# An RWKV-6 scan with a SoLU MLP on one core: exponentials kept in PSUM, the bonus term moved to GpSimd and TensorE, y copied by ScalarE

## The chip, the cores and the metric

The kernel runs on one core of one Trainium2 chip. The metric is the device time of one execution in microseconds (us). Five engines work side by side, each through its own queue in program order: TensorE (PE; its weight loads are listed as PEld), VectorE (DVE), ScalarE (ACT), GpSimd (POOL) and SyncE (SP), which here only sends DMAs. They wait for each other through semaphores.

## The reference

Two stages. The first is a linear attention with a decay per channel, over batch 4, 8 heads, 768 steps and head size 48:

```python
for t in range(S):
    cur = u * k[t] (outer) v[t]
    y[t] = r[t] @ (state + cur)
    state = w[t][:, None] * state + k[t] (outer) v[t]
```

The second takes the 3072 rows of y (384 wide, all heads side by side) through an MLP:

```python
h = x @ w_in                       # 384 -> 1024
solu = h * softmax(h)
ln = (solu - mean) / sqrt(var + 1e-6) * g_ln
out = ln @ w_out                   # 1024 -> 384
```

The term with u is the bonus: for each step and head it is the scalar sum over d of r*u*k, times v.

## The kernel before, in words

The sequence is cut into chunks of 128 steps. A unit is one chunk of one batch entry with all eight heads: 24 units, numbered c*4 + b, so that a state (one per batch entry) is read and written by every fourth unit. Each unit goes through a chain of stages, and the loop over t emits the stages of five neighbouring units together. The functions are emitted in the order of that loop, but the order in which instructions stand on each engine is made by a scheduler; the rows in the section on the change come from the built programs.

The stages of unit i, by function:

- `load(i)`: four DMAs of 192 KB bring w, k, r, v (f32) from SP's queue. The pool `io` holds five of each.
- `decay(i)`: ScalarE takes log w (`lw`, L128), TensorE cumulates it over the 128 steps by two triangular matrices into the PSUM tile `cum_ps` (L130, L131), and ScalarE writes the exponential of both halves to the SBUF tile `ex` in bf16 (L133).
- `scaled(i)`: VectorE multiplies k and r by the two halves, giving `kp` and `rp` (L140, L141).
- `bonus(i)`: GpSimd casts v to bf16 (`vb`, L147), and makes p = r*k (L149) and q = p*u (L151); VectorE sums q over each head (`dg`, L153) and makes `dv` = vb times dg (L155).
- `transposed(i)`: TensorE transposes kp and rp into `kr_ps`, VectorE copies them to `kr` (L165).
- `scores(i)`: TensorE makes k-by-r products in `m_ps` (L175), ScalarE copies them to `m` (L177), GpSimd masks them to the strict triangle (L178).
- `attend(i)`: TensorE sums into `y_ps` the read of the state (L190) and m times vb (L194); VectorE adds dv and writes `y` (L198).
- `state(i)`: TensorE forms the new state in `s_ps` (last matmul L220), ScalarE the decay `et` (L223), VectorE writes `st` (L228).
- `x_transposed(i)` and `hidden(i)`: y is transposed (`x_ps`, `xT`, L237), 24 matmuls make `h_ps` (L246), ScalarE makes e = exp(h) (L249), VectorE he = h*e (L251).
- `output(i)`: TensorE sums he times the prepared second weights into `o_ps` (L261, L264), and he times he into `g_ps` (L263). The statistics follow as a chain of small steps: `sq` on ScalarE (L267), `junk` with its accumulated `ss` on VectorE (L270), `qm` = ss - sq on VectorE (L272), `lv` = log and `rs` = exp(-lv/2) on ScalarE (L274, L276), and the scaled copy `o` (L278), which a DMA on SP's queue stores (L279).

PSUM has eight banks here: the pool `big` has two tiles of two banks, taken in turn by cum_ps, h_ps and m_ps; the pool `small` has four of one bank, taken by kr_ps, y_ps, o_ps, g_ps, x_ps and s_ps. Most SBUF tiles of a stage have three buffers (pool `wk`). Ahead of the loop the constants and the first units are loaded, and `setup_weights` prepares the second weights `w2`: 16 f32 matmul passes (L115) and eight VectorE instructions (L119), after the small DMA of g (`g_sb`, L102) has landed.

Of the kernel before, what the change touches and what calls it, by code (L numbers as in the profile page):

```python
# [9 lines left out]
BF16 = mybir.dt.bfloat16  # L10
AX = mybir.AxisListType.X
EXP = mybir.ActivationFunctionType.Exp
# [8 lines left out]
def kernel(  # L21
# [12 lines left out]
    nc = tc.nc  # L34
    B, H, S, D = r.shape
    C = 128
    NC = S // C
    DM = H * D
# [12 lines left out]
    wk = ctx.enter_context(tc.tile_pool(name="wk", bufs=3))  # L51
# [6 lines left out]
    def load(i):  # L58
        c, b = units[i]
        for name, src in (("w", w), ("k", k), ("r", r), ("v", v)):  # L60
            t = io.tile([C, H, D], F32, tag=name + "_in", name=name + "_in")
            nc.sync.dma_start(out=t, in_=src[b, :, c * C:(c + 1) * C, :].rearrange("h t d -> t h d"))  # L62
            live[i][name] = t
# [12 lines left out]
    ident = consts.tile([C, C], BF16)  # L76
# [14 lines left out]
    for b in range(B):  # L91
        nc.vector.memset(st_t[b], 0.0)

    u_bc = consts.tile([C, H, D], F32)
    nc.sync.dma_start(out=u_bc, in_=u.partition_broadcast(C))
    load(1)
    win_sb = consts.tile([128, KM, DF], BF16)
    nc.gpsimd.dma_start(out=win_sb, in_=moe_w_in.rearrange("(ko ki) f -> ki ko f", ki=128))
    wout_f = consts.tile([128, KF, DM], F32)
# [24 lines left out]
    def decay(i):  # L124
        L = live[i]
        lw = lw_t[i % NR]
        L["lw"] = lw
        nc.scalar.activation(out=lw[:, :, :D], in_=L["w"], func=LN)  # L128
        cum = big.tile([C, 2, 512], F32, tag="b", name="cum_ps")
        nc.tensor.matmul(cum[:, 0, :DM], lhsT=uti_neg, rhs=lw[:, :, :D], start=True, stop=True)  # L130
        nc.tensor.matmul(cum[:, 1, :DM], lhsT=uts, rhs=lw[:, :, :D], start=True, stop=True)  # L131
        ex = wk.tile([C, 2, DM], BF16, tag="ex", name="ex")
        nc.scalar.activation(out=ex, in_=cum[:, :, :DM], func=EXP)  # L133
        L["ex"] = ex

    def scaled(i):
        L = live[i]
        kp, rp = kp_t[i % NR], rp_t[i % NR]
        ex = L["ex"].rearrange("t e (h d) -> t e h d", h=H)
        nc.vector.tensor_mul(out=kp[:, :, :D], in0=L["k"], in1=ex[:, 0])  # L140
        nc.vector.tensor_mul(out=rp[:, :, :D], in0=L["r"], in1=ex[:, 1])  # L141
        L["kp"], L["rp"] = kp, rp

    def bonus(i):
        L = live[i]
        vb = wk.tile([C, H, D], BF16, tag="vb", name="vb")
        nc.gpsimd.tensor_copy(out=vb, in_=L["v"])  # L147
        p = wk.tile([C, H, D], BF16, tag="p", name="p")
        nc.gpsimd.tensor_mul(out=p, in0=L["r"], in1=L["k"])  # L149
        q = wk.tile([C, H, D], BF16, tag="q", name="q")  # L150
        nc.gpsimd.tensor_mul(out=q, in0=p, in1=u_bc)  # L151
        dg = wk.tile([C, H], F32, tag="dg", name="dg")
        nc.vector.reduce_sum(out=dg, in_=q, axis=AX)  # L153
        dv = wk.tile([C, H, D], BF16, tag="dv", name="dv")
        nc.vector.tensor_mul(out=dv, in0=vb, in1=dg.unsqueeze(2).to_broadcast([C, H, D]))  # L155
        L["vb"], L["dv"] = vb, dv

    def transposed(i):
# [23 lines left out]
    def attend(i):  # L182
        L = live[i]
        c, b = units[i]
        m, kr, vb, st = L["m"], L["kr"], L["vb"], st_t[b]
        y_ps = small.tile([C, DM], F32, tag="s", name="y_ps")
        first = True
        if c > 0:
            for hp in range(HP):
                nc.tensor.matmul(y_ps[:, hp * 2 * D:(hp + 1) * 2 * D], lhsT=kr[:, HP + hp, :], rhs=st[:, hp, :],  # L190
                                 start=first, stop=False, skip_group_check=True)
                first = False
        for h in range(H):
            nc.tensor.matmul(y_ps[:, h * D:(h + 1) * D], lhsT=m[:, h % 2, h // 2, :], rhs=vb[:, h, :],  # L194
                             start=first, stop=(h == H - 1), skip_group_check=True)
            first = False
        y = wk.tile([C, DM], BF16, tag="y", name="y")
        nc.vector.tensor_add(out=y, in0=y_ps, in1=L["dv"].rearrange("t h d -> t (h d)"))  # L198
        L["y"] = y

    def state(i):
# [52 lines left out]
    def output(i):  # L254
        L = live[i]
        c, b = units[i]
        e, he = L["e"], L["he"]
        o_ps = small.tile([C, DM + 2], F32, tag="s", name="o_ps")
        g_ps = small.tile([C, C], F32, tag="s", name="g_ps")
        for f in range(KF):  # L260
            nc.tensor.matmul(o_ps[:, :DM + 1], lhsT=he[:, f, :], rhs=w2[:, f, :], start=(f == 0), stop=False,  # L261
                             skip_group_check=True)
            nc.tensor.matmul(g_ps, lhsT=he[:, f, :], rhs=he[:, f, :], start=(f == 0), stop=(f == KF - 1))  # L263
            nc.tensor.matmul(o_ps[:, DM + 1:], lhsT=e[:, f, :], rhs=inv_col, start=False, stop=(f == KF - 1),  # L264
                             skip_group_check=True)
        sq = wk.tile([C, 2], F32, tag="sq", name="sq")
        nc.scalar.activation(out=sq, in_=o_ps[:, DM:], func=SQUARE)  # L267
        junk = wk.tile([C, C], BF16, tag="junk", name="junk")
        ss = wk.tile([C, 1], F32, tag="ss", name="ss")
        nc.vector.scalar_tensor_tensor(out=junk, in0=g_ps, scalar=1.0, in1=ident, op0=MULT, op1=MULT, accum_out=ss)  # L270
        qm = wk.tile([C, 1], F32, tag="qm", name="qm")
        nc.vector.tensor_sub(out=qm, in0=ss, in1=sq[:, 0:1])  # L272
        lv = wk.tile([C, 1], F32, tag="lv", name="lv")
        nc.scalar.activation(out=lv, in_=sq[:, 1:2], func=LN, scale=1e-6 * DF * DF, bias=qm)  # L274
        rs = wk.tile([C, 1], F32, tag="rs", name="rs")
        nc.scalar.activation(out=rs, in_=lv, func=EXP, scale=-0.5)  # L276
        o = io.tile([C, DM], F32, tag="o", name="o")
        nc.scalar.activation(out=o, in_=o_ps[:, :DM], func=COPY, scale=rs)  # L278
        nc.sync.dma_start(out=out[b * S + c * C:b * S + (c + 1) * C, :], in_=o)  # L279
# [5 lines left out]
    for t in range(NU + LAST):  # L285
        on = lambda d: 0 <= t - d < NU
        if t + LOOK < NU:
            load(t + LOOK)
        if on(0):
            decay(t)  # L290
            bonus(t)
        if on(3):
            hidden(t - 3)
        if on(0):
            scaled(t)
        if on(1):
            transposed(t - 1)
        if on(2):
            attend(t - 2)
        if on(4):  # L300
            output(t - 4)
        if on(1):
            scores(t - 1)
        if on(2):
            x_transposed(t - 2)
            state(t - 2)
        if t == 1:
            setup_weights()
# [30 lines left out]
```

## Time and profile before

| | |
|---|---|
| median of 3 runs | 214.92 us (214.33 to 215.04) |
| profiled execution, its own time | 214.99 us |
| its span, first to last instruction | 213.3 us |
| VectorE busy | 161.3 us (76%) |
| TensorE busy | 153.5 us (72%) |
| ScalarE busy | 104.8 us (49%) |
| GpSimd busy | 93.7 us (44%) |

The profile is of one execution, so its 214.99 us are what its rows are summed against. They stand 0.07 us above the median. A busy time counts how long instructions ran, also while they were held up by something inside, so a busy share says which engines are candidates and not which one sets the pace. The chain of waits (which follows the last instruction back to what released each step) and the timelines of single engines tell that.

### The profile page before, as it was taken

What the parts mean: (1) busy time and instruction counts of PE and PEld (TensorE: products, weight loads), DVE (VectorE), ACT (ScalarE), POOL (GpSimd) and SP (SyncE); (2) the same over time, 40 slices, a digit from 0 to 9 for tenths busy, and PEclk for the clock granted to TensorE, in tenths of its full rate; (3) what the DMA queues carried; (4) which work ended last, traced back from release to release, by engine and by line L of the source; (5) the groups of instructions that cost most, each with busy time, mean ns of one, the idle gap of its engine ahead of it and who ended that gap; (6) DMA issues with size and microseconds to landing.
All of it is one profiled execution on the core that took longest, in us unless ns stands there. A gap on an engine that the chain in (4) does not pass through costs nothing.

```text
span 213.3 us, 5315 instructions
## 1 busy us (share of the span) xinstructions
PE 153.5 (72%) x2120; PEld 120.5 (57%) x2120; DVE 161.3 (76%) x338; ACT 104.8 (49%) x213; POOL 93.7 (44%) x108
## 2 busy tenths in 40 slices
PE   1031790758788877976987897897788889899970
PEld 0010450647676655864865576676567767687660
DVE  3037349899989989878888898798898787985420
ACT  3031010445564665474376455547545666665652
POOL 4049254458645364473274367256436331322200
PEclk9999997599799999998899997999996999999999
DMA  6999999992457979786765675485561001010102
GB/s 124 219 200 267 181 182 187 190 175 54 92 94 160 190 139 185 160 167 124 163 148 119 139 150 125 86 173 125 114 148 40 32 11 40 37 39 37 40 37 75
DMA packets 105944, 26.49 MB, mean 124 GB/s; under 512 B 101312, under 2 KB 105536, under 8 KB 105920
## 3 DMA queue, kind: packets, MB, share of 16 engines
q1 hardware_dynamic: 105520, 25.37, 59.5%
q0 software_dynamic: 400, 0.79, 2.0%
q8 instruction: 16, 0.26, 0.5%
q14 instruction: 8, 0.07, 0.1%
HBM read 22.22 MB, written 4.72 MB: 126 GB/s over the span
## 4 chain that ended last, share of the span: by engine, by line
DVE 38%; PE 19%; SPq 12%; issue 10%; ACT 9%; DMA 6%; POOL 3%; POOLq 1%; DVEq 0%; ACTq 0%
SPq L62 10%; DVE he L251 9%; PE h_ps L246 6%; DVE rp L141 6%; PE o_ps L261 5%; DVE kp L140 4%; DVE kr L165 4%; DMA r_in<-in_r_dram 4%; DVE y L198 3%; DVE w L119 2%; DVE dg L153 2%; ACT m L177 2%; DVE st L228 2%; DVE qm L272 2%; DVE dv L155 2%
## 5 line engine op out<-in xcount | busy, mean ns | idle before, releaser
L261 PE MATMUL o_ps<-w,he 128*128 128x385 bf16 x192 | 50.2, 329 | 1.1 <-DVE he L251 1.1
L263 PE MATMUL g_ps<-he 128*128 128x128 bf16 x192 | 41.9, 220 | 0.0
L246 PE MATMUL h_ps<-xT,win_sb 128*128 128x128 bf16 x576 | 40.7, 233 | 0.0
L147 POOL CAST vb<-v_in 128x384 bf16<-128x384 f32 x24 | 12.5, 520 | 63.9 <-PE s_ps L220 54.3
L246 PEld LDWEIGHTS <-win_sb 128*128 128x128 bf16 x576 | 38.5, 106 | 3.4 <-issue 1.0
L178 POOL TENSOR_SCALAR_AFFINE_SELECT m<-m 128x1024 bf16<-128x1024 bf16 x24 | 27.6, 1150 | 23.2 <-ACT m L177 23.0
L149 POOL TENSOR_TENSOR p<-r_in,k_in 128x384 bf16<-128x384 f32 x24 | 25.1, 1047 | 16.5 <-DMA r_in<-in_r_dram 15.6
L249 ACT ACTIVATE e<-h_ps 128x1024 bf16<-128x1024 f32 x24 | 24.6, 1025 | 15.2 <-PE h_ps L246 14.9
L264 PE MATMUL o_ps<-inv_col,e 128*128 128x1 bf16 x192 | 32.0, 167 | 0.0
L251 DVE TENSOR_TENSOR he<-h_ps,e 128x1024 bf16<-128x1024 f32 x24 | 29.1, 1214 | 3.7 <-ACT e L249 3.6
L130 PE MATMUL cum_ps<-lw,uti_neg 128*128 128x384 bf16 x24 | 8.4, 351 | 31.6 <-ACT lw L128 31.4
L177 ACT CAST m<-m_ps 128x1024 bf16<-128x1024 f32 x24 | 24.0, 999 | 13.8 <-PE m_ps L175 13.8
L151 POOL TENSOR_TENSOR q<-p,u_bc 128x384 bf16<-128x384 bf16 x24 | 26.2, 1095 | 1.6
L140 DVE TENSOR_TENSOR kp<-k_in,ex 128x384 bf16<-128x384 f32 x24 | 16.4, 685 | 13.3 <-ACT ex L133 13.1
L264 PEld LDWEIGHTS <-e 128*128 128x128 bf16 x192 | 18.7, 97 | 13.1 <-issue 0.9
L133 ACT ACTIVATE ex<-cum_ps 128x768 bf16<-128x768 f32 x24 | 19.4, 808 | 11.8 <-PE cum_ps L131 9.0
L141 DVE TENSOR_TENSOR rp<-r_in,ex 128x384 bf16<-128x384 f32 x24 | 22.6, 941 | 0.0
L131 PEld LDWEIGHTS <-uts 128*128 128x128 bf16 x24 | 2.3, 97 | 32.6 <-issue 32.5
L155 DVE TENSOR_TENSOR dv<-vb,dg 128x384 bf16<-128x384 bf16 x24 | 15.9, 663 | 5.3 <-POOL vb L147 5.0
L261 PEld LDWEIGHTS <-he 128*128 128x128 bf16 x192 | 18.8, 98 | 1.5 <-DVE he L251 1.4
L128 ACT ACTIVATE lw<-w_in 128x384 bf16<-128x384 f32 x24 | 12.5, 519 | 12.8 <-DMA w_in<-in_w_dram 12.8
L263 PEld LDWEIGHTS <-he 128*128 128x128 bf16 x192 | 18.4, 96 | 0.1
(59 smaller groups left out, 271.3 us busy)
## 6 DMA issues: line engine op xcount, KB each, us to landing
w_in<-in_w_dram SPq DMA_DIRECT2D x24, 192.0 KB, 4.3
k_in<-in_k_dram SPq DMA_DIRECT2D x24, 192.0 KB, 3.9
r_in<-in_r_dram SPq DMA_DIRECT2D x24, 192.0 KB, 3.8
v_in<-in_v_dram SPq DMA_DIRECT2D x24, 192.0 KB, 3.9
out_dram<-o SPq DMA_DIRECT2D x24, 192.0 KB, 2.0
wout_f<-in_moe_w_out_dram SPq DMA_DIRECT2D x1, 1536.0 KB, 9.1
win_sb<-in_moe_w_in_dram POOLq DMA_DIRECT2D x1, 768.0 KB, 8.4
u_bc<-in_u_dram SPq DMA_DIRECT2D x1, 192.0 KB, 8.4
```

Source lines behind the costliest of these rows:

```text
L140: nc.vector.tensor_mul(out=kp[:, :, :D], in0=L["k"], in1=ex[:, 0])
L141: nc.vector.tensor_mul(out=rp[:, :, :D], in0=L["r"], in1=ex[:, 1])
L149: nc.gpsimd.tensor_mul(out=p, in0=L["r"], in1=L["k"])
L151: nc.gpsimd.tensor_mul(out=q, in0=p, in1=u_bc)
L177: nc.scalar.copy(out=m, in_=m_ps)
L178: nc.gpsimd.affine_select(out=m, in_=m, compare_op=ALU.is_gt, fill=0.0, base=0, pattern=[[0, H], [1, C]], channel_multiplier=-1)
L246: nc.tensor.matmul(h_ps[:, f, :], lhsT=win_sb[:, j, f * 128:(f + 1) * 128], rhs=L["xT"][:, j, :], start=(j == 0), stop=(j == KM - 1))
L249: nc.scalar.activation(out=e, in_=h_ps, func=EXP)
L251: nc.vector.tensor_mul(out=he, in0=h_ps, in1=e)
L261: nc.tensor.matmul(o_ps[:, :DM + 1], lhsT=he[:, f, :], rhs=w2[:, f, :], start=(f == 0), stop=False, skip_group_check=True)
L263: nc.tensor.matmul(g_ps, lhsT=he[:, f, :], rhs=he[:, f, :], start=(f == 0), stop=(f == KF - 1))
L264: nc.tensor.matmul(o_ps[:, DM + 1:], lhsT=e[:, f, :], rhs=inv_col, start=False, stop=(f == KF - 1), skip_group_check=True)
```

## The change

It has five parts. (1) The exponentials of the cumulated decays are written back, in f32, into the PSUM tile cum_ps that held the logarithms, and kp and rp read them there. The SBUF tile ex is gone. (2) dv is made by GpSimd. (3) dv enters y_ps by a matmul with the identity, as the first of the sum; ScalarE then copies y_ps to y, in place of VectorE's addition. (4) qm is made by GpSimd. (5) At the start the four loads of unit 1 are sent ahead of the load of u.

```diff
+    load(1)
     u_bc = consts.tile([C, H, D], F32)
     nc.sync.dma_start(out=u_bc, in_=u.partition_broadcast(C))
-    load(1)
...
-        ex = wk.tile([C, 2, DM], BF16, tag="ex", name="ex")
-        nc.scalar.activation(out=ex, in_=cum[:, :, :DM], func=EXP)
-        L["ex"] = ex
+        nc.scalar.activation(out=cum[:, :, :DM], in_=cum[:, :, :DM], func=EXP)
+        L["ex"] = cum
...
-        ex = L["ex"].rearrange("t e (h d) -> t e h d", h=H)
-        nc.vector.tensor_mul(out=kp[:, :, :D], in0=L["k"], in1=ex[:, 0])
-        nc.vector.tensor_mul(out=rp[:, :, :D], in0=L["r"], in1=ex[:, 1])
+        ex = L["ex"][:, :, :DM].rearrange("t e (h d) -> t e h d", h=H)
+        nc.vector.tensor_mul(out=kp[:, :, :D], in0=ex[:, 0], in1=L["k"])
+        nc.vector.tensor_mul(out=rp[:, :, :D], in0=ex[:, 1], in1=L["r"])
...
-        nc.vector.tensor_mul(out=dv, in0=vb, in1=dg.unsqueeze(2).to_broadcast([C, H, D]))
+        nc.gpsimd.tensor_mul(out=dv, in0=vb, in1=dg.unsqueeze(2).to_broadcast([C, H, D]))
...
-        first = True
+        nc.tensor.matmul(y_ps, lhsT=ident, rhs=L["dv"].rearrange("t h d -> t (h d)"), start=True, stop=False,
+                         skip_group_check=True)
         if c > 0:
...
-        nc.vector.tensor_add(out=y, in0=y_ps, in1=L["dv"].rearrange("t h d -> t (h d)"))
+        nc.scalar.copy(out=y, in_=y_ps)
...
-        nc.vector.tensor_sub(out=qm, in0=ss, in1=sq[:, 0:1])
+        nc.gpsimd.tensor_sub(out=qm, in0=ss, in1=sq[:, 0:1])
```

VectorE, one period in the middle of the loop (the kp of unit 13), before:

```order
L153 TENSOR_REDUCE dg<-q 128x8
L140 TENSOR_TENSOR kp_98<-k_in,ex 128x8x48
L141 TENSOR_TENSOR rp_101<-r_in,ex 128x8x48
L198 TENSOR_TENSOR y<-y_ps,dv 128x384
L251 TENSOR_TENSOR he<-h_ps,e 128x1024
L270 SCALAR_TENSOR_TENSOR junk,ss<-g_ps,ident 128x128
L272 TENSOR_TENSOR qm<-ss,sq 128x1
L237 COPY xT<-x_ps 128x384
L155 TENSOR_TENSOR dv<-vb,dg 128x384
L228 TENSOR_TENSOR st_115<-s_ps,et 64x4x48 x2
L165 COPY kr<-kr_ps 128x1024
```

The same engine and place in the changed kernel, whose line numbers are one or two lower:

```order
L152 TENSOR_REDUCE dg<-q 128x8
L139 TENSOR_TENSOR kp_98<-cum_ps,k_in 128x8x48
L140 TENSOR_TENSOR rp_101<-cum_ps,r_in 128x8x48
L249 TENSOR_TENSOR he<-h_ps,e 128x1024
L268 SCALAR_TENSOR_TENSOR junk,ss<-g_ps,ident 128x128
L235 COPY xT<-x_ps 128x384
L164 COPY kr<-kr_ps 128x1024
L226 TENSOR_TENSOR st_115<-s_ps,et 64x4x48 x2
```

y, qm and dv are gone from VectorE, kp and rp read cum_ps, and he stands directly behind rp. The dg at the head of the period belongs to a unit three ahead of the kp behind it.

GpSimd in the middle of the loop, before, one period with the q ahead of it:

```order
L151 TENSOR_TENSOR q<-p,u_bc 128x384
L147 CAST vb<-v_in 128x384
L178 AFFINE_SELECT m<-m 128x1024
L149 TENSOR_TENSOR p<-r_in,k_in 128x384
L151 TENSOR_TENSOR q<-p,u_bc 128x384
```

And in the changed kernel:

```order
L150 TENSOR_TENSOR q<-p,u_bc 128x384
L270 TENSOR_TENSOR qm<-ss,sq 128x1
L146 CAST vb<-v_in 128x384
L154 TENSOR_TENSOR dv<-vb,dg 128x384
L177 AFFINE_SELECT m<-m 128x1024
L148 TENSOR_TENSOR p<-r_in,k_in 128x384
L150 TENSOR_TENSOR q<-p,u_bc 128x384
```

qm stands behind p and q of a unit eight ahead of its own, and dv stands between vb (its own unit) and the mask of a unit two behind.

ScalarE, one period of the changed kernel (before, the same row without the y, and with ex in place of the second name of cum_ps):

```order
L132 ACTIVATE cum_ps<-cum_ps 128x2x384
L247 ACTIVATE e<-h_ps 128x1024
L196 CAST y<-y_ps 128x384
L265 ACTIVATE sq<-o_ps 128x2
L272 ACTIVATE lv<-sq,qm 128x1
L176 CAST m<-m_ps 128x1024
L274 ACTIVATE rs<-lv 128x1
L221 ACTIVATE et<-s_ps 128x4
L128 ACTIVATE lw_96<-w_in 128x8x48
L276 ACTIVATE o<-o_ps,rs 128x384
```

The copy of y stands between e and sq. lv, which waits for qm, still stands ahead of m, et and the next unit's lw.

## Rows read from the trace of the kernel before

**Rows 1.** The page's busy times, then a stretch of windows (PE, PEld, DVE, ACT, POOL).

```profile
PE 153.5 (72%) x2120; PEld 120.5 (57%) x2120; DVE 161.3 (76%) x338; ACT 104.8 (49%) x213; POOL 93.7 (44%) x108
...
130.00:160.00 30.00, 25.03 (x360) 20.19 (x360) 26.34 (x52) 16.66 (x35) 15.40 (x16) 0.94 0.62 131
```

**Rows 2.** Chain that ended last, middle of the loop: start us, us, what.

```profile
117.71 1.19 DVE rp L141
118.90 0.47 DVE y L198
...
120.81 0.42 DVE qm L272
...
125.14 1.20 DVE rp L141
```

**Rows 3.** The same chain near the end, after GpSimd's last p and q.

```profile
175.42 0.32 PE cum_ps L130
...
175.90 1.35 PE h_ps L246 x24
...
177.28 1.03 ACT e L249
...
178.34 1.23 DVE he L251
...
179.87 0.17 DVE qm L272
...
181.89 0.32 PE cum_ps L130
```

**Rows 4.** Single lines: instructions, min/median/max ns, first and last start.

```profile
L140 DVE TENSOR_TENSOR kp<-k_in,ex x24: 545/554/1361, 14.1 to 188.2; 128x384 bf16<-128x384 f32 x24
...
L141 DVE TENSOR_TENSOR rp<-r_in,ex x24: 545/1266/1279, 14.6 to 188.8; 128x384 bf16<-128x384 f32 x24
...
L198 DVE TENSOR_TENSOR y<-y_ps,dv x24: 542/550/558, 38.5 to 200.0; 128x384 bf16<-128x384 f32 x24
...
L272 DVE TENSOR_TENSOR qm<-ss,sq x24: 149/160/806, 53.2 to 208.8; 128x1 f32<-128x1 f32 x24
...
L151 POOL TENSOR_TENSOR q<-p,u_bc x24: 915/1112/1306, 16.0 to 162.4; 128x384 bf16<-128x384 bf16 x24
...
L278 ACT ACTIVATE o<-o_ps,rs x24: 577/579/582, 54.9 to 209.6; 128x384 f32<-128x384 f32 x24
```

**Rows 5.** Timeline from 123.3 us, GpSimd's q and VectorE's rp.

```profile
124.67 1.25 POOL L151 TENSOR_TENSOR q<-p,u_bc 128x384 bf16<-128x384 bf16 x1
...
125.06 1.28 DVE L141 TENSOR_TENSOR rp<-r_in,ex 128x384 bf16<-128x384 f32 x1
```

**Rows 6.** Timelines of ScalarE, GpSimd and VectorE: three waits (idle before, releaser).

```profile
127.11 0.17 ACT L267 ACTIVATE sq<-o_ps 128x2 f32<-128x2 f32 x1 [1.14 <-PE o_ps L264]
...
173.94 0.50 POOL L147 CAST vb<-v_in 128x384 bf16<-128x384 f32 x1 [4.37 <-PE s_ps L220]
...
21.82 0.17 DVE L108 TENSOR_SCALAR gr<-g_sb 128x8 f32<-128x8 f32 x1 [1.25 <-DMA g_sb<-in_moe_g_ln_dram]
```

**Rows 7.** Timeline of VectorE: y of unit 0, kp of units 3 and 20.

```profile
38.54 0.54 DVE L198 TENSOR_TENSOR y<-y_ps,dv 128x384 bf16<-128x384 f32 x1
...
42.60 0.85 DVE L140 TENSOR_TENSOR kp<-k_in,ex 128x384 bf16<-128x384 f32 x1 [0.43 <-ACT ex L133]
...
170.47 0.55 DVE L140 TENSOR_TENSOR kp<-k_in,ex 128x384 bf16<-128x384 f32 x1
```

**Rows 8.** Granted clock in 40 slices, windows at 102 us, the chain there.

```profile
PEclk9999997599799999998899997999996999999999
...
102.00:103.00 1.00, 1.00 (x13) 1.00 (x11) 1.00 (x1) 0.00 (x0) 0.75 (x1) 0.50 0.83 183
...
101.04 2.51 PE h_ps L246 x24
```

**Rows 9.** GpSimd's waits from 45 to 100 us: total, times, longest.

```profile
POOL p L149 <- DMA r_in<-in_r_dram: 5.5, 3, 2.7
```

More of the change, by code (lines that the diff above doesn't have):

```diff
@@ L190, in attend @@
                 nc.tensor.matmul(y_ps[:, hp * 2 * D:(hp + 1) * 2 * D], lhsT=kr[:, HP + hp, :], rhs=st[:, hp, :],
-                                 start=first, stop=False, skip_group_check=True)
-                first = False
+                                 start=False, stop=False, skip_group_check=True)
         for h in range(H):
             nc.tensor.matmul(y_ps[:, h * D:(h + 1) * D], lhsT=m[:, h % 2, h // 2, :], rhs=vb[:, h, :],
-                             start=first, stop=(h == H - 1), skip_group_check=True)
-            first = False
+                             start=False, stop=(h == H - 1), skip_group_check=True)
         y = wk.tile([C, DM], BF16, tag="y", name="y")
-        nc.vector.tensor_add(out=y, in0=y_ps, in1=L["dv"].rearrange("t h d -> t (h d)"))
+        nc.scalar.copy(out=y, in_=y_ps)
         L["y"] = y
```

## The prediction

> **What bounds the kernel now.** I read the page's busy times first. VectorE leads with 161.3 us of the span, TensorE follows with 153.5 us, GpSimd has the least of the four, 93.7 us [rows 1]. No engine is full, so I went on to the chain of waits in the middle of the loop. There the reader is to see one period, from one rp to the next: 125.14 - 117.71 = 7.43 us. Nearly all of its long steps are VectorE's, and two of them are odd [rows 2]. An rp takes 1.19 us there, and a qm, which handles one column, 0.42 us.
>
> The views of single lines say why. kp and rp are the same operation on the same shapes, and their shortest runs are equal, 545 ns; but rp's median is 1266 ns and kp's longest run is 1361 ns. qm runs from 149 to 806 ns. y, with one operand in PSUM, stays between 542 and 558 ns in all its 24 runs [rows 4]. So something holds up VectorE's instructions with two operands in SBUF and leaves alone those with one in PSUM. The timeline shows what: GpSimd's q ran from 124.67 for 1.25 us, to 125.92, and the rp that started at 125.06 ended at 126.34, 0.42 us after q did [rows 5]. rp did its work when q was over. q paid as well: 1.25 us there, 915 ns at its shortest [rows 4].
>
> Near the end, when GpSimd has no p and q left, the same chain looks different [rows 3]. It goes from cum_ps through h_ps on TensorE, e on ScalarE, he, junk and qm on VectorE, and through lv, m, et and lw on ScalarE to the next cum_ps. he (178.34) begins where e (177.28 + 1.03) ends, so VectorE no longer lags. That period lasts 181.89 - 175.42 = 6.47 us, with the state, dv and y still in it. It is the loop that remains when VectorE is punctual.
>
> **The change part by part.** *kp and rp read PSUM.* Neither then has two operands in SBUF, so each should take what y takes. The shortest run is kept, and the hold of 1266 - 545 = 721 ns on rp goes. For a PSUM operand in place of one in SBUF the bounds are nothing and, by the longest y against the shortest kp, 13 ns; I take nothing.
>
> The Trainium skill's page "VectorE: DVE Perf Modes", section "The TRN2 errata", speaks against this: its cost table gives 58 cycles of fixed cost to an instruction that reads SBUF and 120 to one that reads PSUM, 65 ns more at its 0.96 GHz. By that rule, as an estimate, two instructions in each of 17 periods would add up to 2.2 us to the sum below if VectorE set the pace; by the rows of y and kp [rows 4] they add nothing.
>
> ScalarE now writes its exponentials to PSUM. No row shows such a write. ScalarE waits after it in any case, so I take no change; the bounds are 0.2 us less and 0.3 us more a period, of which the second would show only if e came later. The tile is now held until rp has read it. The next user of these banks is m_ps, which stands behind all of o_ps on TensorE, and so behind a he that VectorE starts after rp.
>
> *y, dv and qm leave VectorE.* y's 0.47 us and qm's 0.42 us stood on the chain [rows 2]. On ScalarE the copy of y costs about what o costs, 579 ns for the same size out of PSUM [rows 4]. It lies between e and sq, where ScalarE now idles 1.14 us for o_ps [rows 6], and x_ps, which needs it, stands behind o_ps too. If that cover went, it would cost 17 x 0.58 = 9.9 us. The identity matmul has the size of one cum_ps matmul, 0.32 us as listed [rows 3], and TensorE is idle 30 - 25.03 = 4.97 us in 30 [rows 1]; it stands ahead of cum_ps, which waits for ScalarE's lw. I take nothing; without that cover it costs at most 17 x 0.32 = 5.4 us.
>
> *GpSimd takes dv and qm.* Now it is busy 15.40 us in 30 [rows 1], 3.81 us a period; without q's hold (1.25 - 0.92) some 3.5 us. For dv there is no row on this engine. The bounds are 0.54 us, what VectorE takes unhindered for such a product (kp), and 1.31 us, the longest q. I take the shortest q, 0.92 us, which has the same size, two operands and the same output type. For qm I take 0.2 us, between 0.15 us and 0.8 us (VectorE's own range); the loop then has 0.05 us more in each period than in rows 3. The whole comes to 4.6 us a period. What matters is the order. A period on GpSimd starts with vb, which waits for s_ps and began at 173.94 in the loop's last form [rows 6], and qm was wanted at 179.87 [rows 3]: 5.93 us for work of 4.4 us. So qm is not late, with 1.5 us to spare.
>
> A new wait comes with it. dg has three buffers, so VectorE's dg, at the head of its row, waits until GpSimd's dv of three units earlier has read the old one. Behind it are queued kp, rp and he, and TensorE waits for these. That dv is over 0.50 + 0.92 us after vb's start, at 175.36 in the terms of rows 3, while kp can't start before the exponential of the cum_ps begun at 175.42. dg itself then runs while cum_ps and the exponential do. If dv came later than that, kp, rp and m_ps would be late one for one.
>
> *u is loaded later.* SP's queue sends the same things. In the start VectorE idled 1.25 us for the small DMA of g [rows 6], which stays behind the same bytes, and the weight set-up follows from it. I take nothing for this, between 0 and 1 us either way.
>
> *The start.* y of unit 0 stood on VectorE behind the eight instructions of the weight set-up and ran at 38.54; x_ps, s_ps and the cum_ps of unit 3 followed, and kp of unit 3 began at 42.60 [rows 7]. On ScalarE y needs only y_ps. What is left between them is kr, m_ps, m and the exponential. I put kp of unit 3 at 41.0, with a gain of 1.6 us (bounds 0 and 2.5).
>
> **The sum.** Between the kp of units 3 and 20 lie 17 periods, 170.47 - 42.60 = 127.87 us, 7.52 us each [rows 7]. They are to become 6.47 us: 17 x 1.05 = 17.9 us less. Against that stands TensorE's clock. The page's slices show dips of the granted clock about once in 30 us of the loop; at 102 us it was 0.50, which is 1.2 GHz, and h_ps took 2.51 us [rows 8] against 1.35 us [rows 3], 1.16 us more. Rows 3 has no such fall. In the new loop h_ps is on the path, so each costs 1.16 us; I allow three, 3.5 us, with bounds of none and five (5.8 us). qm on GpSimd: 17 x 0.05 = 0.9 us. The start gives 1.6 us. The end stays, since its loop is already that of rows 3. So 214.99 - 17.9 + 3.5 + 0.9 - 1.6 = 199.9, say **200.0 us**. The median of the runs is 0.07 us below the profiled execution, which changes nothing.
>
> **The rivals.** (a) *Late loads and a slow clock eat half.* From 45 to 100 us GpSimd's p waited 5.5 us for r [rows 9]. Those waits hid behind VectorE's lag. Now qm stands behind p and q in GpSimd's queue, and behind qm all of ScalarE's row. If all 5.5 us come through, and five falls of the clock (2.3 us more), the time is 207.8 us. For it: units come faster, so the loads have less time. Against: the DMA engines are 0.62 busy at 131 GB/s in the middle [rows 1], and 131 x 7.43/6.47 = 150 GB/s leaves room.
>
> (b) *GpSimd becomes the bound, and the kernel slower.* Nothing shows dv's operand, one value repeated over 48 columns, on GpSimd. If it ran at a fraction of q's rate, its length would go straight into qm and from there into lv, m and lw. The spare 1.5 us covers a dv of 2.4 us. It takes a dv of 2.4 + 1.05 = 3.5 us to lose what the loop gained, and at 4.2 us each period is 0.7 us longer than before: 214.99 + 17 x 0.7 - 1.6 = 225 us. Against it: VectorE's kp and GpSimd's q, 545 and 915 ns, differ by less than a factor of two.
>
> (c) *A better end.* No fall of the clock in the loop, a GpSimd qm as short as VectorE's, and the start at its better bound: 214.99 - 17.9 - 2.5 = 194.6 us.
>
> (d) *Nothing comes of it*, because VectorE is held up by GpSimd in the new form too, or another chain of 7.4 us stands behind. The steady 542 to 558 ns of y [rows 4] speaks against the first, rows 3 against the second. With the start at its lower bound that is 214.99 us.
>
> **How the numbers follow.** I give 0.60 to the forecast (196 to 204 us), 0.18 to (a), 0.10 to (c), 0.08 to (b) and 0.04 to (d). The range from **194.5 to 207.5 us** takes in the forecast, most of (c) and nearly all of (a). About what this measurement can tell from no change is 0.3%, 0.64 us. Faster by more than that: 0.60 + 0.18 + 0.10 = 0.88; within it (most of d): 0.03; slower: 0.08 + 0.01 = 0.09.
>
> **What the new profile would show.** Right: kp and rp near 0.55 us in all 24 runs, and q near 0.92 us; a VectorE busy time near 114 us (24 x (0.55 + 0.55 + 0.16 + 0.72) = 47.5 us less, for y, dv, qm and the hold); periods of about 6.5 us, in which he starts when e ends; the chain passing through e, he, qm, m and lw. Wrong: a dv on GpSimd far above 1 us, an m or qm that ScalarE waits for because GpSimd is still in p or q, VectorE waiting for dv at dg, or a granted clock of 0.50 in many more periods.

## The result, and the profile after

The changed kernel takes 202.7 us (median of 4 runs, 202.34 to 203.94), the kernel before beside it 214.98 us (214.33 to 215.34). The ratio is 0.944, with a 95% interval from 0.940 to 0.949. The profiled execution took 202.66 us, its span 201.0 us, 12.3 us less than before.

The page of the changed kernel, busy times and granted clock:

```profile
PE 149.8 (75%) x2144; PEld 117.3 (58%) x2144; DVE 118.7 (59%) x266; ACT 113.3 (56%) x237; POOL 110.3 (55%) x156
...
PEclk9999999559999999999999999999999999999997
```

A stretch of its windows, columns as in rows 1:

```profile
130.00:160.00 30.00, 26.96 (x430) 22.04 (x428) 21.48 (x46) 21.08 (x45) 18.14 (x25) 1.00 0.50 112
```

VectorE fell from 161.3 to 118.7 us, 76% to 59% of the span [rows 1], and the time by only 5.6%. The granted clock, which fell about once in 30 us before [rows 8], does not fall in the loop after 45 us. In the single lines (min/median/max ns, as in rows 4) the hold on kp and rp is gone:

```profile
L139 DVE TENSOR_TENSOR kp<-cum_ps,k_in x24: 545/558/560, 13.3 to 175.3; 128x384 bf16<-128x384 f32 x24
...
L140 DVE TENSOR_TENSOR rp<-cum_ps,r_in x24: 542/548/548, 13.8 to 175.8; 128x384 bf16<-128x384 f32 x24
...
L150 POOL TENSOR_TENSOR q<-p,u_bc x24: 912/916/1112, 18.0 to 151.0; 128x384 bf16<-128x384 bf16 x24
...
L154 POOL TENSOR_TENSOR dv<-vb,dg x24: 826/828/830, 20.2 to 171.3; 128x384 bf16<-128x384 bf16 x24
...
L196 ACT CAST y<-y_ps x24: 473/473/479, 32.0 to 187.5; 128x384 bf16<-128x384 f32 x24
...
L270 POOL TENSOR_TENSOR qm<-ss,sq x24: 189/189/192, 51.2 to 196.5; 128x1 f32<-128x1 f32 x24
```

rp's median is 548 ns, from 1266 [rows 4]. During 18 of its 24 runs a p, a q or the mask of m was under way on GpSimd for at least a part of the time, and none of the 24 was longer than 548 ns.

The chain in the steady part of the loop (start us, us, what), one period from cum_ps to cum_ps:

```profile
116.29 0.32 PE cum_ps L130
...
116.77 1.35 PE h_ps L244 x24
...
118.15 1.03 ACT e L247
...
119.20 0.04 DVE he L249
119.24 1.06 issue
...
120.35 0.30 DVE junk L268 x2
...
120.78 0.20 POOL qm L270
...
121.00 0.29 ACT lv L272
121.30 0.06 ACT m L176
121.36 0.74 issue
...
122.36 0.42 ACT lw L128
...
122.83 0.32 PE cum_ps L130
```

It is the loop of rows 3, and he starts when e ends. The two long pieces named "issue" cover the rest of he (1.23 us in all) and of m. The period is 122.83 - 116.29 = 6.54 us, 0.07 us more than in rows 3.

From 54 to 105 us it is not like that. The timelines of GpSimd and VectorE there:

```profile
94.83 0.99 POOL L148 TENSOR_TENSOR p<-r_in,k_in 128x384 bf16<-128x384 f32 x1 [1.41 <-DMA r_in<-in_r_dram]
...
98.16 0.83 POOL L154 TENSOR_TENSOR dv<-vb,dg 128x384 bf16<-128x384 bf16 x1
...
62.48 0.55 DVE L152 TENSOR_REDUCE dg<-q 128x8 f32<-128x384 bf16 x1 [2.24 <-POOL q L150]
63.07 0.56 DVE L139 TENSOR_TENSOR kp<-cum_ps,k_in 128x384 bf16<-128x384 f32 x1
...
99.02 0.55 DVE L152 TENSOR_REDUCE dg<-q 128x8 f32<-128x384 bf16 x1 [3.46 <-POOL dv L154]
99.60 0.56 DVE L139 TENSOR_TENSOR kp<-cum_ps,k_in 128x384 bf16<-128x384 f32 x1
```

p waited 1.41 us for r; vb, q, m and dv stood behind it; dg needed the buffer that this dv read, and waited 3.46 us at the head of VectorE's row; kp began 0.58 us after dg. The period before that kp was 9.6 us. The one that ended at 63.07 was 9.05 us: there dg waited for a q that stood behind vb, dv, m and p.

### The profile page after: what moved, and what is told of

It reads as the page before. It is cut to its first block, busy times and chain, and to the rows that moved or that the text cites. A ratio compares the mean times of both kernels' runs of the same rounds, so it can differ in the third digit from the quotient of the medians.

```text
span 201.0 us, 5426 instructions
## 1 busy us (share of the span) xinstructions
PE 149.8 (75%) x2144; PEld 117.3 (58%) x2144; DVE 118.7 (59%) x266; ACT 113.3 (56%) x237; POOL 110.3 (55%) x156
## 4 chain that ended last, share of the span: by engine, by line
PE 27%; ACT 15%; issue 14%; DVE 13%; POOL 12%; DMA 11%; SPq 6%; POOLq 0%; DVEq 0%
PE h_ps L244 10%; DMA r_in<-in_r_dram 7%; ACT e L247 6%; SPq L62 5%; DMA g_sb<-in_moe_g_ln_dram 5%; PE o_ps L259 5%; PE m_ps L115 4%; DVE he L249 3%; DVE w L119 3%; POOL m L177 3%; ACT lw L128 3%; DVE junk L268 2%; POOL p L148 2%; POOL q L150 2%; PE cum_ps L130 2%
## 5 line engine op out<-in xcount | busy, mean ns | idle before, releaser
L249 DVE TENSOR_TENSOR he<-h_ps,e 128x1024 bf16<-128x1024 f32 x24 | 29.3, 1221 | 15.8 <-ACT e L247 15.8
L244 PEld LDWEIGHTS <-win_sb 128*128 128x128 bf16 x576 | 35.3, 100 | 4.1 <-issue 1.4
L244 PE MATMUL h_ps<-xT,win_sb 128*128 128x128 bf16 x576 | 37.2, 223 | 0.5 <-ACT m L176 0.5
L270 POOL TENSOR_TENSOR qm<-ss,sq 128x1 f32<-128x1 f32 x24 | 4.5, 190 | 48.5 <-DVE junk L268 48.5
L139 DVE TENSOR_TENSOR kp<-cum_ps,k_in 128x384 bf16<-128x384 f32 x24 | 13.4, 557 | 20.5 <-ACT cum_ps L132 20.4
L152 DVE TENSOR_REDUCE dg<-q 128x8 f32<-128x384 bf16 x24 | 13.3, 552 | 19.7 <-POOL q L150 15.3
L132 ACT ACTIVATE cum_ps<-cum_ps 128x768 f32<-128x768 f32 x24 | 19.1, 797 | 9.8 <-PE cum_ps L131 7.7
L150 POOL TENSOR_TENSOR q<-p,u_bc 128x384 bf16<-128x384 bf16 x24 | 22.2, 925 | 3.5 <-DMA u_bc<-in_u_dram 1.8
L154 POOL TENSOR_TENSOR dv<-vb,dg 128x384 bf16<-128x384 bf16 x24 | 19.8, 828 | 5.4 <-DVE dg L152 4.3
L164 DVE COPY kr<-kr_ps 128x1024 bf16<-128x1024 bf16 x24 | 16.6, 690 | 8.6 <-PE kr_ps L162 8.3
L128 ACT ACTIVATE lw<-w_in 128x384 bf16<-128x384 f32 x24 | 12.5, 520 | 15.6 <-DMA w_in<-in_w_dram 15.1
L259 PEld LDWEIGHTS <-he 128*128 128x128 bf16 x192 | 18.6, 97 | 1.3 <-DVE he L249 1.2
```

The costliest lines, as they stand in the source:

```text
L132: nc.scalar.activation(out=cum[:, :, :DM], in_=cum[:, :, :DM], func=EXP)
L154: nc.gpsimd.tensor_mul(out=dv, in0=vb, in1=dg.unsqueeze(2).to_broadcast([C, H, D]))
L244: nc.tensor.matmul(h_ps[:, f, :], lhsT=win_sb[:, j, f * 128:(f + 1) * 128], rhs=L["xT"][:, j, :], start=(j == 0), stop=(j == KM - 1))
L249: nc.vector.tensor_mul(out=he, in0=h_ps, in1=e)
```

## The experiments

Times are medians, with the ratio to the kernel before on the same chip. The changed kernel's ratio is 0.944.

**One part alone, and all but that part.** The kernel before with only the exponentials in PSUM:

```
-        ex = wk.tile([C, 2, DM], BF16, tag="ex", name="ex")
-        nc.scalar.activation(out=ex, in_=cum[:, :, :DM], func=EXP)
+        nc.scalar.activation(out=cum[:, :, :DM], in_=cum[:, :, :DM], func=EXP)
...
-        nc.vector.tensor_mul(out=rp[:, :, :D], in0=L["r"], in1=ex[:, 1])
+        nc.vector.tensor_mul(out=rp[:, :, :D], in0=ex[:, 1], in1=L["r"])
```

> The kernel before with the first part of the change alone: the exponentials go back into PSUM and kp and rp read them there; y, dv and qm stay on VectorE. Theory A (the gain comes from ending GpSimd's hold on kp and rp, and he is punctual once it is gone): kp and rp at 0.55 us in all 24 runs, VectorE busy near 144 us, the period near 6.6 us, the time 203 to 207 us, most of the 12 us. Theory B (the hold only moves on to the next instruction with two operands in SBUF, dv or qm, and the load of y, dv and qm on VectorE is what counted): kp and rp short, but dv or qm longer by several tenths of a us than before, and 209 to 214 us.

It took 201.16 us, ratio 0.934 (0.928 to 0.939): as fast as the whole change or faster. The page's busy times, and the same stretch of windows:

```profile
PE 149.6 (75%) x2120; PEld 117.4 (59%) x2120; DVE 156.7 (79%) x338; ACT 105.9 (53%) x213; POOL 88.6 (45%) x108
```

```profile
130.00:160.00 30.00, 27.42 (x416) 21.61 (x414) 29.17 (x62) 20.53 (x44) 13.68 (x17) 1.00 0.46 105
```

Both theories missed. The time is below A's range, but by another way: VectorE is busy 29.17 of 30 us, and the chain there is VectorE's alone, 6.44 us from kp (123.87) to kp (130.31). And B's move of the hold did happen: dv's median rose from 558 to 1240 ns. The holder is GpSimd's mask of m, by the timelines of both engines:

```profile
126.94 1.09 POOL L177 TENSOR_SCALAR_AFFINE_SELECT m<-m 128x1024 bf16<-128x1024 bf16 x1
...
127.19 1.25 DVE L154 TENSOR_TENSOR dv<-vb,dg 128x384 bf16<-128x384 bf16 x1
```

dv ended at 128.44, 0.41 us after m at 128.03, as rp ended 0.42 us after q in rows 5.

That the moved hold costs so little has a reason in the kernel before. Its period was not VectorE's row alone: from qm the chain went over lv, m, rs and et on ScalarE, and VectorE stood still 0.69 us in front of st until et was there. The first line is from there, the second from the same place here, without the wait:

```profile
122.65 0.72 DVE L228 TENSOR_TENSOR st<-s_ps,et 64x192 bf16<-64x192 f32 x2 [0.69 <-ACT et L223]
...
128.37 0.72 DVE L227 TENSOR_TENSOR st<-s_ps,et 64x192 bf16<-64x192 f32 x2
```

From the start of rp to that of dv VectorE now takes 2.86 us in place of 3.79 (rp and qm are shorter), and from the start of dv to that of kr 1.92 in place of 2.00: the 0.7 us by which dv is held fill the time that VectorE had waited for et. So VectorE's busy time falls by only 4.6 us, and the time by some 14.

The changed kernel with ex and both products back in SBUF (the diff above reversed, the rest as changed):

> The changed kernel with that part undone: ex is an SBUF tile again, and kp and rp read it there; everything else as changed. Theory A: rp's median goes back above 1 us, he is late in each period again, 207 to 211 us. Theory B (the load of y, dv and qm was what counted): rp is long again but the loop has room for it, 201 to 204 us.

It took 208.82 us, ratio 0.970 (0.963 to 0.977), as theory A has it: the later periods are 6.8 to 7.2 us, and rp is held again.

```profile
L141 DVE TENSOR_TENSOR rp<-r_in,ex x24: 545/1266/1360, 14.3 to 181.7; 128x384 bf16<-128x384 f32 x24
```

So the parts do not add up: 6.6% for the exponentials alone, 3.0% for the rest without them, 5.6% together.

**What holds VectorE.** The kernel before, with GpSimd's two products as copies:

```
-        nc.gpsimd.tensor_mul(out=p, in0=L["r"], in1=L["k"])
+        nc.gpsimd.tensor_copy(out=p, in_=L["r"])
-        nc.gpsimd.tensor_mul(out=q, in0=p, in1=u_bc)
+        nc.gpsimd.tensor_copy(out=q, in_=p)
```

> The kernel before, in which GpSimd makes p as a copy of r and q as a copy of p, one operand each in place of two, so the bonus term is left out of the result; kp, rp, dv and qm read SBUF as before. Theory A (what holds VectorE's instructions with two SBUF operands is GpSimd's instructions with two SBUF operands): rp at 0.55 us and qm at 0.15 us in nearly all runs although ex is in SBUF, the period 6.4 to 6.6 us, 199 to 205 us. Theory B (any SBUF work of GpSimd holds them, a copy too): rp's median stays above 0.9 us, 210 to 215 us.

It took 198.86 us, ratio 0.924 (0.917 to 0.931). Theory A has the period of 6.5 us and the medians of rp (551 ns) and qm (160 ns); the time is just under its range. Its mechanism is wrong. Where a copy is under way when rp starts, rp is held as in rows 5:

```profile
40.71 0.92 POOL L151 COPY q<-p 128x384 bf16<-128x384 bf16 x1
...
41.18 0.86 DVE L141 TENSOR_TENSOR rp<-r_in,ex 128x384 bf16<-128x384 f32 x1
```

rp ended at 42.04, 0.41 us after the copy at 41.63. All four rp that started during a copy took 0.85 or 0.86 us. The copies take 510 ns (median of q) in place of 1112, so that most are over when rp starts. In these rows a GpSimd instruction with one SBUF operand holds as one with two does; the mask of m, with one, does it too. The Trainium skill says as much in "SBUF — State Buffer", section "Who interferes with whom": a VectorE instruction with two SBUF inputs contends with a GpSimd instruction that reads SBUF, for ports that only one of them can have at a time, and the order of issue decides who waits. The rows here agree, with the held instruction ending 0.41 or 0.42 us after the holder.

**The other parts, one by one.** Three kernels, each the changed one with one line as before or on VectorE:

```
+        nc.vector.tensor_sub(out=qm, in0=ss, in1=sq[:, 0:1])
...
+        nc.vector.tensor_mul(out=dv, in0=vb, in1=dg.unsqueeze(2).to_broadcast([C, H, D]))
...
+        nc.vector.tensor_copy(out=y, in_=y_ps)
```

> The changed kernel with qm back on VectorE. Theory A (the 4 us that units 3 to 12 lose come in through qm, which stands behind p and q on GpSimd, so that a late r holds up lv and all behind it): 198 to 200 us, the time from the kp of unit 3 to that of unit 12 falls from 63.3 us to 60 or less, and the steady period from 6.54 to about 6.45 us. Theory B (the late r comes in through dg, which stands at the head of VectorE's row ahead of kp; qm's place makes no difference): 201.5 to 203.5 us, and the same stretch of 62 to 64 us.

199.52 us, ratio 0.926 (0.921 to 0.932). A has the time, the steady period is 6.47 us, and the stretch from unit 3 to 12 fell to 61.1 us, between the two theories. The profiled stretch from the kp of unit 20 to the end is 43.3 us, against 44.1 in the changed kernel. So, by these two profiles, GpSimd's qm cost the changed kernel 0.07 us in a steady period, 1.6 us more in that stretch (63.3 - 61.1 less 9 x 0.07) and 0.8 us at the end. Of the two worst periods one fell, from 9.60 to 8.14 us; the other did not (9.05 and 9.02 us).

> The changed kernel with dv back on VectorE, so that dg waits for no GpSimd instruction but q. Theory A (dv on GpSimd is no gain while the loop of waits sets the period, and its 0.83 us stands in GpSimd's row ahead of m, p, q and qm, where the stretch of units 3 to 12 loses its time): the steady period stays within 0.1 us of 6.54, that stretch falls from 63.3 us to 61 to 62.5 us, 199 to 202 us. Theory B (dv on VectorE, held by q to 1.2 us, makes st, dg or kp late): period above 6.65 us, 204 to 206 us.

203.93 us, ratio 0.951 (0.946 to 0.955), a little slower than changed, on the edge of what can be told. The steady period is 6.54 us as A said, but the stretch did not shrink (63.7 us), so A is wrong in that: dv is not what loses time there by itself. B's hold of 1.2 us did not come: dv's median is 559 ns.

> The changed kernel with the copy of y on VectorE in place of ScalarE (the bonus is still added by the identity matmul). Theory A (y lies beside other work on either engine): 202 to 204 us, steady period 6.5 to 6.6 us. Theory B (y ahead of he in VectorE's row makes he late by up to its 0.47 us in each period): 207 to 211 us, period 6.8 to 7.0 us.

201.41 us, ratio 0.938 (0.934 to 0.943). The steady period is 6.54 us: y fills VectorE's wait before he, which fell from 15.8 to 3.8 us in the whole execution, and costs nothing. That speaks for A. The time is just under its range, because the stretch from unit 3 to 12 took 59.0 us in this order of the work; the start was 1.6 us later. One period of 9.0 us is left in that stretch (74.02 to 83.02), the others are 6.6 us or less. Why this order has only one was not followed further.

```
-    load(1)
     u_bc = consts.tile([C, H, D], F32)
     nc.sync.dma_start(out=u_bc, in_=u.partition_broadcast(C))
+    load(1)
```

> The changed kernel with u loaded ahead of unit 1 again, as before the change. Theory A (the order of that load changes nothing that the end sees): within 0.7 us of the changed kernel, 202 to 203.4 us, kp of unit 3 at 41.5 to 42.3 us. Theory B (GpSimd's q of unit 0 waits 1.8 us for u in the changed kernel, and that is why the start gave 0.7 us where 1.6 was forecast): 200.5 to 202 us, kp of unit 3 near 41 us.

202.55 us, ratio 0.943 (0.939 to 0.947): no change, as A has it. kp of unit 3 starts at 42.37 us, just behind A's 42.3.

**Late loads.** The changed kernel with the loads' buffers from five to eight and the look-ahead from three units to five:

```
-    io = ctx.enter_context(tc.tile_pool(name="io", bufs=5))
+    io = ctx.enter_context(tc.tile_pool(name="io", bufs=8))
-    LOOK = 3
+    LOOK = 5
```

> The changed kernel with eight buffers for each load in place of five, and loads issued five units ahead in place of three. Theory A (r comes late because its load is issued late, behind SP's waits for the stores and for free buffers): GpSimd's waits for r vanish from 45 to 100 us, units 3 to 12 take 6.6 us each, 198 to 200 us. Theory B (r comes late because the DMA engines are full in that stretch, whatever the order of issue): waits for r of the same sum, 201.5 to 203.5 us.

202.78 us, ratio 0.942 (0.935 to 0.948). A's waits for r from 45 to 100 us did vanish (2.6 us in the changed kernel, none here), and the stretch fell by 2.0 us to 61.3, but the time did not: one later period of 7.8 us (117.49 to 125.27) and a start 1.3 us later took it back. In that period dg waited 1.71 us for a dv that stood behind p and m in GpSimd's row, with no load late. The first of the worst periods stays as well, 8.81 us in place of 9.05. So late loads are a part of the loss in the stretch, and not the whole.

**Cutting the loop.** ScalarE's log is emitted one unit ahead, with a fourth buffer, on top of the deep loads; the same with qm on VectorE; the same on the kernel with the exponentials in PSUM alone:

```
-    def decay(i):
-        L = live[i]
-        lw = lw_t[i % NR]
+    def logs(i):
+        L = live[i]
+        lw = lw_t[i % NL]
         L["lw"] = lw
         nc.scalar.activation(out=lw[:, :, :D], in_=L["w"], func=LN)
+
+    def decay(i):
+        L = live[i]
+        lw = L["lw"]
...
         if on(0):
             decay(t)
             bonus(t)
+        if t + 1 < NU:
+            logs(t + 1)
```

> The changed kernel with the deep loads of loads_deep and with ScalarE's lw computed one unit ahead (four buffers for lw), so that cum_ps no longer waits for lv, m, rs and et of its own period. Theory A (the steady period of 6.54 us is a loop of waits, cum_ps, h_ps, e, he, junk, qm, lv, m, et, lw, and no engine is full): the loop is cut, TensorE with its 5.9 us a period becomes the bound, the period falls to 5.9 to 6.2 us and the time to 192 to 196 us. Theory B (the period is set elsewhere, by an engine's whole row or by a free PSUM buffer behind m): 6.4 to 6.55 us as before, 201 to 203 us.

> The same with qm on VectorE. Theory A: the period as in the run beside it (qm is no longer on a loop that decides), 191 to 195 us. Theory B: 6.4 to 6.5 us a period, 198 to 200 us.

> The kernel with the exponentials in PSUM alone (y, dv and qm on VectorE), with deep loads and lw one unit ahead. Theory A (there VectorE's row is full, 29.2 us of 30, and no loop decides): the period stays at 6.40 to 6.45 us and the time at 199 to 202 us, whatever is done to lw; what y, dv and qm on other engines are worth shows only once the loop is cut, as the difference to the two runs beside this one, 5 to 8 us. Theory B (its 6.44 us is the same loop of waits as in the changed kernel): it falls as they do, to 193 to 197 us.

195.25 us (0.908, 0.902 to 0.914), 193.54 us (0.899, 0.891 to 0.907) and 201.86 us (0.939, 0.932 to 0.945). Theory A holds in the first two, which fall to periods of 6.14 and 6.02 us. The third does not gain, and its time is in A's range, but not for A's reason: its period grew from 6.44 to 6.75 us, dv is held longer (median 1422 ns in place of 1240) and waits 0.43 us for vb in each period, and the chain there goes from VectorE's y over x_ps and s_ps on TensorE and vb on GpSimd back to dv. So a loop of waits does decide there, another than the one that was cut. That dv:

```profile
120.10 1.42 DVE L161 TENSOR_TENSOR dv<-vb,dg 128x384 bf16<-128x384 bf16 x1 [0.43 <-POOL vb L153]
```

Windows of the second and the third kernel, in this order:

```profile
100.00:130.00 30.00, 28.25 (x450) 23.08 (x448) 23.32 (x55) 21.46 (x50) 22.12 (x27) 1.00 0.87 166
```

```profile
100.00:130.00 30.00, 25.56 (x410) 20.96 (x408) 28.05 (x58) 19.28 (x41) 19.75 (x21) 1.00 0.69 143
```

In one TensorE is nearly full (28.25 of 30), in the other VectorE is the busiest (28.05). Moving y, dv and qm off VectorE is worth 201.86 - 195.25 = 6.6 us here, and nothing while the loop stood.

The last kernel takes the second of these and sends the store of o from ScalarE's queue, since the load of r that was late at 139 us had stood behind a store on SP's:

```
-        nc.sync.dma_start(out=out[b * S + c * C:b * S + (c + 1) * C, :], in_=o)
+        nc.scalar.dma_start(out=out[b * S + c * C:b * S + (c + 1) * C, :], in_=o)
```

> The kernel of logs_ahead_deep_qmv (changed kernel, qm on VectorE, lw one unit ahead, deep loads), with the store of o issued from ScalarE's queue in place of SP's. Theory A (what is left of late loads comes from SP's row: in that run the load of r that GpSimd waited for until 139.07 us stood behind a store that waited for o until 135.16 us): GpSimd's waits for r from 45 us on sum to less than 1 us, no period of 7 us or more after 60 us, 190 to 192.5 us. Theory B (the DMA engines are the limit, 0.87 busy there): the waits come back elsewhere, 193 to 195 us.

191.85 us, ratio 0.894 (0.890 to 0.898), the lowest of all; its interval overlaps that of the kernel that it was made from (0.891 to 0.907), so the gain of this step is not clear. From 45 us on GpSimd never waits for r. Two periods of 7.0 and 7.2 us remain, against the expectation. TensorE is busy 28.82 of 30 us:

```profile
130.00:160.00 30.00, 28.82 (x457) 23.46 (x455) 23.05 (x54) 22.65 (x50) 13.19 (x18) 1.00 0.09 34
```

## Why the prediction was right, point by point

The forecast of 200.0 us was 2.7 us too low, and the time lies inside its range. Its mechanism holds for the steady periods: VectorE is punctual, and the loop of rows 3 sets the pace. The starts of kp in the changed kernel give the terms one by one (unit 3, then unit 20):

```profile
41.88 0.55 DVE L139 TENSOR_TENSOR kp<-cum_ps,k_in 128x384 bf16<-128x384 f32 x1
...
156.87 0.56 DVE L139 TENSOR_TENSOR kp<-cum_ps,k_in 128x384 bf16<-128x384 f32 x1 [0.47 <-ACT cum_ps L132]
```

| term | predicted, us | measured, us |
|---|---|---|
| 17 periods at 6.47 in place of 7.52 | -17.9 | -17.9, the base of the next rows |
| qm on GpSimd, a period | 0.05: +0.9 | 0.07: +1.2 |
| falls of the clock | +3.5 | 0 |
| disturbed periods, 3 to 14 | 0 (rival a: +5.5) | +3.8 |
| start, to the kp of unit 3 | -1.6 | -0.7 |
| end, from the kp of unit 20 | 0 | +1.3 |
| sum | -15.1 | -12.3 |

The fifth row is 156.87 - 41.88 = 114.99 us less 17 x 6.54 = 111.18.

**Right.** *kp and rp*: their medians, 558 and 548 ns with an operand in PSUM, are within 13 ns of the shortest runs of rows 4. The 65 ns that I had estimated from "VectorE: DVE Perf Modes" of the Trainium skill (section "The TRN2 errata") are not there. *exp into PSUM*: 797 ns on average, no loss. *dv* at 828 ns (taken 0.92), *qm* at 189 ns (taken 0.2), *the copy of y* at 473 ns (taken 579), hidden; the run with y on VectorE has the same steady period. *The order of u*: nothing. *The loop of rows 3*: the run with qm on VectorE reproduces its 6.47 us. *qm is not late*: GpSimd stood waiting for VectorE's junk in front of every one of the 24, so none came behind a p or q that was still running:

```profile
L270 POOL TENSOR_TENSOR qm<-ss,sq 128x1 f32<-128x1 f32 x24 | 4.5, 190 | 48.5 <-DVE junk L268 48.5
```

The other side of it is that the next vb, dv, m, p and q in GpSimd's row stand behind that wait as long as there are any left to run (48.5 us in the whole execution).

**Mis-sized.** *The clock.* I allowed three falls at 1.16 us; none came after 45 us.

*The wait of dg for dv*, taken as hidden; it is one of the signs of being wrong that I had named. It is hidden from unit 14 on. Earlier, dg waited 4.1 us for dv in two periods and 8.2 us for q in seven (40 to 160 us); not all of that reached the end, 3.8 us did. This is rival (a) in part, but it reached kp through dg at the head of VectorE's row at 99.02, where I had put it into qm. The late r begins one of the two worst periods; the other, at 63.07, needs no late load, only a q that stands last in GpSimd's row. Deep loads took 2.0 us off the stretch and qm back on VectorE took 2.2 us off it, 0.6 of these in steady cost; neither removed the period that ends at 63.07. What else sets the stretch stays open.

*The start.* y of unit 0 did run earlier, at 32.03 us in place of 38.54 [rows 7]. I had overlooked that the kp of unit 2 stands on VectorE behind the weight set-up too, and kr, m_ps and unit 3's cum_ps behind it:

```profile
32.34 5.43 DVE w L119 x7
37.77 0.48 DVE kp L139
```

*The end.* I took its loop to be that of rows 3 in the old kernel already. The kp of units 20 to 23 before lie 6.31, 6.47 and 4.97 us apart, the new ones 6.54, 6.54 and 5.40; qm on GpSimd is 0.8 us of the 1.3.

*VectorE's busy time*, put near 114 us, is 118.7. By single lines y, dv, qm, kp and rp lost 48.6 us, near the 47.5 of the forecast; but neighbouring instructions of VectorE overlap by some 0.08 us (kp from 117.16 for 0.55 us, rp from 117.62), and the page's busy time counts such a stretch once.

The clock and the disturbed periods nearly cancel, 3.5 against 3.8 us. That is luck: the forecast is nearer to the result than its terms are.

**What the prediction did not ask.** It took the change as one. The exponentials in PSUM alone give the whole gain: VectorE, no longer held at rp, gets through its row in 6.44 us, since the hold moves to dv, into time that VectorE had spent waiting for et. The other parts then take 29.17 - 21.48 = 7.7 us in 30 off an engine whose row is about as long as the loop behind it, and the loop does not move. The part of VectorE's 42.6 us that the time did not follow is waiting now, 15.8 us of it in front of he.

## What to carry to other kernels

Where one instruction has two durations, look at what another engine has under way at its start; cutting that overlap (an operand in PSUM, a shorter or earlier instruction there) can be worth more than moving the instruction. The hold may come back at the next such instruction; what counts is whether the engine had been waiting there anyway. When the busiest engine's row and a loop of waits are about equally long, relief of either shows nothing until the other is cut, so try the parts of a change singly and together. An engine that is handed work brings its place in line with it: qm, 0.19 us long, cost 202.7 - 199.5 = 3.2 us there.

## What the runs showed of the hardware

A GpSimd instruction with one SBUF operand held VectorE's two-operand instructions as those with two did: the mask of m (dv 1.25 us for 0.55), a copy (rp 0.86 us). VectorE's products with one operand in PSUM were never held: kp and rp of the changed kernel took 542 to 560 ns in 48 of 48 runs, 35 of them with a p, a q or the mask under way on GpSimd.

In the kernel before, the granted clock fell to 0.50 (1.2 GHz) four times in the loop; in the fall of rows 8 TensorE had stood nearly idle just before, busy 0.04 us from 99 to 100 us, and the clock was 0.50 from 100 to 103 us. In the changed kernel it did not fall after 45 us, though TensorE was as idle there once, busy 0.09 us from 97 to 98 us. The stretches of 30 us do not tell them apart either: the clock was 0.94 on average with TensorE busy for 25.03 us [rows 1], and 1.00 with 24.60 us in the changed kernel from 75 to 105 us. Why it fell in the one and not in the other, no run here tells.
